# Two reciprocals of a linear-attention layer: one VectorE instruction each in place of two on ScalarE

## The chip, the core and the metric

The kernel runs on one core of a Trainium2 chip. The metric is the device time of one execution in microseconds (us). The engines are named as in the profile: PE is TensorE's matmuls and PEld its weight loads, DVE is VectorE, ACT is ScalarE, POOL is GpSimd, and SP is the engine that issues most of the transfers. Each engine has its own queue and runs it in order; a semaphore holds an instruction back until what it reads is there.

## The reference

Four layers are applied in turn to `x` (2048 rows of 512, bf16), A B A B, each as `x = x + layer(layernorm(x))`. Layer A is a linear attention with 32 heads of 16:

```
pq = einsum("bhsd,hdf->bhsf", q, w_phi);  pk likewise
phi_q = concat[softmax(pq), softmax(-pq)]      # 32 features a head
phi_k = concat[softmax(pk), softmax(-pk)]
kv  = einsum("bhsf,bhsd->bhfd", phi_k, v);  z = einsum("bhsf->bhf", phi_k)
num = einsum("bhqf,bhfd->bhqd", phi_q, kv)
den = einsum("bhqf,bhf->bhq", phi_q, z) + 1e-6
o = num / den;  return o @ wo
```

Layer B is a sliding attention over 8 positions that lie 2 apart (logits, softmax, weighted sum of v, `@ wo`). The change touches layer A alone: the divisor of the query's softmax (the query normaliser) and `den` (the denominator).

## The kernel before

The 2048 rows are four blocks of 512 (`b` = 0 to 3), and layers A and B exist twice (`L` = 0, 1). The class `_Fast` builds every layer from short steps. For layer A these are:

- `s_a1`: keys and values of a block; exponentials `Ek` on ACT (L599), their sums over 16 features on DVE (L626 to L639), the reciprocal `rk` on ACT (L645, L646), the scaling of `Ek` on DVE (L651), and the sum over all rows into `kv` on PE (L668).
- `s_a2`: queries of a block; `mq` (L698) and the exponentials `Eq` of both signs on ACT (L706). `ms` (L714) sums the exponentials of a head into the PSUM tile `S`, 128 partitions by 2 signs times 128 rows, and `rs` (L718 to L722) makes `rS` = 1/S of it, f32.
- `s_akv`: once a layer, when all four blocks have added to `kv`: it is copied (L190 on DVE or L192 on ACT), transposed (L744) and masked into `ZM` and `R` on DVE (L753, L757).
- `s_a3`: `md` (L782) multiplies the exponentials by `ZM` into a PSUM tile; `dr` (L787 to L793) multiplies it by `rS` (L790) and adds the two signs (L793) into `Ds`; `ln` (L795 to L797) makes 1/(Ds + 1e-6); `rho` (L799 to L801) is the product of `rS` and that, which scales the exponentials of the query: for blocks 0 and 1 through PE (`bc`, L808, into PSUM) and DVE (`mulp`, L816), for blocks 2 and 3 through DRAM (`wr`, `rdb`) and DVE (`muld`, L835).
- `s_a4`: `num` on PE (`mo`, L900), its evictions (L190, L192), the product with `wo` (L520), the residual (L533 on DVE, or L523 with L530 on ACT), the squares for the next normalisation (L540), and the normalisation itself (L428 to L444).

Both reciprocals are exp(-ln(x)) on ACT. No step runs in the order in which it is written: a table of 1452 entries, `_ORDER`, says which step is issued next. It fixes the queue of every engine, so the place of a step in the table is its place in the queue of whichever engine it names. The tables `_SLOTS` fix which of 8 PSUM banks and which SBUF buffers each tile takes, so a step also waits until the bank's previous reader is done.

In the table, the four `rs` steps of the first layer A stand behind the scaling of `Ek` of block 2 (block 0), behind `rho` of block 0 (block 1), among the `mulp` of block 1 (block 2) and behind three normalisations L444 of block 0 (block 3). Those of the second layer A stand behind the L651 of block 1 (block 0), behind the sums of block 2 (block 1), between the copy of `kv` and `ZM` (block 2) and among the `mulp` of block 0 (block 3). `ln` stands close behind `dr` each time: directly so for block 0 in both layers, and then `rho` follows at once.

Of the kernel before, what the change touches and what calls it, by code (L numbers as in the profile page):

```python
# [11 lines left out]
ALU = mybir.AluOpType  # L12
ACT = mybir.ActivationFunctionType
# [3 lines left out]
P = 128  # L17
# [8 lines left out]
DEN_EPS = 1e-6  # L26
# [103 lines left out]
class _Fast:  # L130
# [558 lines left out]
    def s_a2(self, L, b):  # L689
        nc, add = self.nc, self.step  # L690
        st = "a2_%d%d" % (L, b)
        T = {}

        def mq(hb):
            xnT = self.xnT["A%d" % L, b]
            T[hb] = pq = self.ps()
            for k in range(NB):
                nc.tensor.matmul(pq[:], lhsT=self.WA[:, k, hb * P:(hb + 1) * P], rhs=xnT[:, :, k, :],  # L698
                                 start=(k == 0), stop=(k == NB - 1))

        def eq(hb, s):
            if (L, b) not in self.Eq:
                self.Eq[L, b] = {}
            if s not in self.Eq[L, b]:
                self.Eq[L, b][s] = self.med([4, NB, P], "Eq")
            nc.scalar.activation(out=self.Eq[L, b][s][:, :, hb, :], in_=T[hb][:].rearrange("p (t i) -> p t i", t=4),  # L706
                                 func=ACT.Exp, scale=1.0 - 2.0 * s)

        def ms():
            T["S"] = S = self.ps()  # L710
            for s in range(2):
                for hb in range(NB):
                    for t in range(4):
                        nc.tensor.matmul(S[32 * t:32 * t + 32, s * P:(s + 1) * P], lhsT=self.indS[:, hb, :],  # L714
                                         rhs=self.Eq[L, b][s][:, t, hb, :], start=(hb == 0 and s == 0),
                                         stop=(hb == NB - 1), tile_position=(0, 32 * t), skip_group_check=True)

        def rs():  # L718
            r = self.sm([2, P], "rS", F32, 4)
            nc.scalar.activation(out=r[:], in_=T["S"][:, 0:2 * P], func=ACT.Ln)  # L720
            nc.scalar.activation(out=r[:], in_=r[:], func=ACT.Exp, scale=-1.0)
            self.rS[L, b] = r  # L722

        for hb in range(NB):
            add(st, "PE", mq, hb)
            add(st, "ACT", eq, hb, 0)
            add(st, "ACT", eq, hb, 1)
        add(st, "PE", ms)
        add(st, "ACT", rs)

    def s_akv(self, L):
# [39 lines left out]
    def s_a3(self, L, b, dma):  # L771
        nc, add = self.nc, self.step
        st = "a3_%d%d" % (L, b)
        zm = self.ZM[L]
        T = {}
# [11 lines left out]
        def dr():  # L787
            r = self.rS[L, b]
            T["DR"] = self.sm([2, P], "s1", F32, 1)
            nc.vector.tensor_tensor(out=T["DR"][:], in0=T["D"][:, 0:2 * P].rearrange("p (s i) -> p s i", s=2),  # L790
                                    in1=r[:], op=ALU.mult)
            T["Ds"] = self.sm([P], "Ds", F32, 1)
            nc.vector.tensor_tensor(out=T["Ds"][:], in0=T["DR"][:, 0, :], in1=T["DR"][:, 1, :], op=ALU.add)  # L793

        def ln():  # L795
            nc.scalar.activation(out=T["Ds"][:], in_=T["Ds"][:], func=ACT.Ln, bias=self.deneps_t[:, 0:1])
            nc.scalar.activation(out=T["Ds"][:], in_=T["Ds"][:], func=ACT.Exp, scale=-1.0)  # L797

        def rho():  # L799
            T["rho"] = self.sm([2, P], "rho", BF16)  # L800
# [35 lines left out]

        add(st, "PE", md)
        add(st, "DVE", dr)
        add(st, "ACT", ln)
        add(st, "DVE", rho)  # L840
        def bev(s, t, direct):
# [397 lines left out]
class _Layout:  # L1239
# [6 lines left out]
    def add(self, name, nelem, nbuf=1):  # L1246
        self.regions[name] = (self.off, nelem, nbuf)
        self.off += nelem * nbuf
        return self
# [568 lines left out]
```

## Time and profile before

| | before |
|---|---|
| device time, median of two runs | 329.95 us (329.52 to 330.39) |
| span of the profiled execution | 327.5 us |
| its own time, taken as the span and the 2.45 us by which the median exceeds it | 329.95 us |
| mean granted TensorE clock | 0.998 |
| busy: PE / DVE / ACT / POOL | 310.3 / 302.2 / 279.3 / 25.3 us |

The span runs from the first to the last instruction of the profiled execution; what starts and ends an execution lies around it. "Busy" is the time in which an engine has an instruction under way. Two layers A take about 0 to 85 us and 170 to 230 us, with parts of layers B beside them; the rest is layer B. A row of the groups gives the source line, engine, operation, output and inputs, their shapes, the count, the busy sum in us and the mean in ns, and behind the last bar the idle time of the engine just before these instructions, with what ended it. A row of the timeline gives the start in us, the length in us and then the same, with the idle time in brackets.

### The profile page before, as it was taken

How to read it: one execution, taken by the hardware profiler on the slowest of the kernel's cores; microseconds unless marked ns; L12 is line 12 of the kernel's file. 1: busy time of each engine (PE TensorE's matmuls, PEld its weight loads, DVE VectorE, ACT ScalarE, POOL GpSimd, SP SyncE). 2: the span in 40 equal slices, each digit the busy share in tenths (PEclk: the TensorE clock that was granted, in tenths of full speed). 3: DMA queues.
4: the chain of work that ended last, by engine and by line, in shares of the span. 5: the costliest groups of instructions: out<-in, count | busy, mean ns of one | idle time of the engine just before them, and what ended most of it. 6: DMA issues, size and time to landing. Idle time of an engine off the chain costs nothing. (4 is left out here: it accounts for less than half of the span.)

```text
span 327.5 us, 8033 instructions
## 1 busy us (share of the span) xinstructions
PE 310.3 (95%) x3176; PEld 149.5 (46%) x3203; DVE 302.2 (92%) x439; ACT 279.3 (85%) x634; POOL 25.3 (8%) x50
## 2 busy tenths in 40 slices
PE   7999999999999999999999999979999999999873
PEld 3655456445444444443444455644544454433221
DVE  7998995998998999899999999699999999999993
ACT  5999988998888999989999999798999996676550
POOL 4000000000021003000000000000000208400000
PEclk9999999999999999999999999999999999999999
DMA  7980000004556899998750300023436977679952
GB/s 197 380 197 3 0 2 4 2 20 120 105 148 135 152 164 133 139 121 154 137 135 1 67 3 2 4 59 90 128 58 125 179 146 134 150 139 158 166 176 92
DMA packets 37388, 35.41 MB, mean 108 GB/s; under 512 B 23008, under 2 KB 32224, under 8 KB 37344
## 3 DMA queue, kind: packets, MB, share of 16 engines
q1 hardware_dynamic: 36816, 34.81, 53.6%
q8 instruction: 27, 0.44, 0.6%
q14 instruction: 17, 0.14, 0.2%
q10 hardware_dynamic: 528, 0.02, 0.1%
HBM read 10.50 MB, written 2.36 MB: 39 GB/s over the span
## 5 line engine op out<-in xcount | busy, mean ns | idle before, releaser
L927 PE MATMUL ps<-xnT,WB 128*128 128x512 bf16 x384 | 87.6, 380 | 0.5 <-DMA xnT<-xn 0.5
L1081 DVE TENSOR_TENSOR pav<-PT,Vg 128x4096 bf16<-128x4096 bf16 (+1 forms) x34 | 72.0, 2162 | 1.5 <-DMA Vg<-V 1.0
L1019 DVE TENSOR_TENSOR prod<-QT,K 128x4096 bf16<-128x4096 bf16 x32 | 72.5, 2291 | 0.3 <-ACT QT L192 0.2
L927 PEld LDWEIGHTS <-WB 128*128 128x128 bf16 x384 | 42.3, 114 | 43.3 <-issue 5.8
L520 PEld LDWEIGHTS <-oT 128*128 128x128 bf16 x256 | 23.8, 97 | 34.5 <-ACT oT L192 5.7
L192 ACT CAST oT<-ps 128x512 bf16<-128x512 f32 (+1 forms) x60 | 32.1, 587 | 8.4 <-PE ps L1090 7.1
L706 ACT ACTIVATE Eq<-ps 128x512 bf16<-128x512 f32 x64 | 34.0, 615 | 0.7 <-PE ps L698 0.6
L520 PE MATMUL ps<-WoB,oT 128*128 128x512 bf16 x122 | 32.1, 380 | 2.4 <-ACT oT L192 2.0
L599 ACT ACTIVATE Ek<-ps 128x512 bf16<-128x512 f32 x64 | 33.6, 622 | 0.4 <-PE ps L593 0.2
L698 PE MATMUL ps<-xnT,WA 128*128 128x512 bf16 x128 | 30.7, 380 | 0.6 <-DVE Eq L816 0.6
L540 ACT ACTIVATE sqd<-x 128x512 bf16<-128x512 bf16 x48 | 30.1, 643 | 1.0 <-DVE x L533 0.8
L605 PE MATMUL ps<-WA,xnT 128*128 128x512 bf16 x120 | 30.0, 380 | 0.5 <-issue 0.2
L593 PE MATMUL ps<-WA,xnT 128*128 128x512 bf16 x124 | 29.7, 380 | 0.6 <-DMA xnT<-xn 0.2
L520 PE MATMUL ps<-WoA,oT 128*128 128x512 bf16 x120 | 29.2, 380 | 0.4
L533 DVE SCALAR_TENSOR_TENSOR x<-ps,x 128x512 bf16<-128x512 f32 x38 | 25.4, 686 | 1.9 <-PE ps L520 1.7
L192 ACT CAST V<-ps 128x512 bf16<-128x512 f32 x31 | 17.5, 595 | 4.4 <-PE ps L927 4.3
L192 ACT CAST K<-ps 128x512 bf16<-128x512 f32 x31 | 17.8, 585 | 3.7 <-PE ps L927 3.3
L530 ACT ACTIVATE x<-ps 128x512 bf16<-128x512 f32 x26 | 15.1, 598 | 6.4 <-PE ps L523 6.3
L192 ACT CAST QT<-ps 128x512 bf16<-128x512 f32 x29 | 17.1, 592 | 2.5 <-PE ps L927 2.5
L651 DVE TENSOR_TENSOR Ek<-Ek,rk 128x4096 bf16<-128x4096 bf16 (+1 forms) x10 | 18.6, 1858 | 0.5 <-ACT rk L646 0.5
L593 PEld LDWEIGHTS <-xnT 128*128 128x128 bf16 x128 | 12.1, 97 | 15.4 <-DMA xnT<-xn 0.7
L446 ACT ACTIVATE xn<-x,nmr,rstd 128x512 bf16<-128x512 bf16 x23 | 18.2, 822 | 1.0 <-DVE nmr L435 0.8
(129 smaller groups left out, 433.3 us busy)
## 6 DMA issues: line engine op xcount, KB each, us to landing
Vg<-V SPq DMA_DIRECT2D x128, 131.5 KB, 4.4
Prho<-rd SPq DMA_DIRECT2D x8, 512.0 KB
x<-in_A_x_dram SPq DMA_DIRECT2D x3, 512.0 KB
WB<-in_B_wqkv_dram SPq DMA_DIRECT2D x3, 512.0 KB, 11.6
wraw<-in_A_wqkv_dram SPq DMA_DIRECT2D x4, 256.0 KB, 4.5
out_dram<-x SPq DMA_DIRECT2D x4, 256.0 KB, 2.2
out_dram<-x SPq DMA_DIRECT2D x8, 128.0 KB, 2.2
x<-in_A_x_dram SPq DMA_DIRECT2D x4, 128.0 KB
```

The lines of the kernel that those rows point to most:

```text
L192: self.nc.scalar.copy(out=out, in_=in_)
L520: nc.tensor.matmul(y[:], lhsT=oT[:, c, t * P:(t + 1) * P], rhs=Wo()[:, c, :], start=(c == 0), stop=(c == NB - 1 and not onpe))
L533: nc.vector.scalar_tensor_tensor(out=xb[:, t, :], in0=T[t][:], scalar=1.0, in1=xb[:, t, :], op0=ALU.mult, op1=ALU.add, **kw)
L540: nc.scalar.activation(out=sqd[:], in_=xb[:, t, :], func=ACT.Square, accum_out=T["ss"][:, t:t + 1])
L593: nc.tensor.matmul(pk[:], lhsT=xnT[:, t, k, :], rhs=self.WA[:, k, D:2 * D], start=(k == 0), stop=(k == NB - 1))
L599: nc.scalar.activation(out=T["E"][:, t, s, :], in_=T["k", t][:], func=ACT.Exp, scale=1.0 - 2.0 * s)
L605: nc.tensor.matmul(pv[:], lhsT=xnT[:, t, k, :], rhs=self.WA[:, k, 2 * D:3 * D], start=(k == 0), stop=(k == NB - 1))
L698: nc.tensor.matmul(pq[:], lhsT=self.WA[:, k, hb * P:(hb + 1) * P], rhs=xnT[:, :, k, :], start=(k == 0), stop=(k == NB - 1))
L706: nc.scalar.activation(out=self.Eq[L, b][s][:, :, hb, :], in_=T[hb][:].rearrange("p (t i) -> p t i", t=4), func=ACT.Exp, scale=1.0 - 2.0 * s)
L927: nc.tensor.matmul(pp[:], lhsT=self.WB[:, k, i * D + c:(i + 1) * D:NB], rhs=xnT[:, :, k, :], start=(k == 0), stop=(k == NB - 1))
L1019: nc.vector.tensor_tensor(out=pr[:], in0=QT[:, c:c + 1, :].to_broadcast([P, NW, TB]), in1=win, op=ALU.mult)
L1081: nc.vector.tensor_tensor(out=pv, in0=PT[:, :, lo:lo + n].unsqueeze(1).to_broadcast([P, NB, 2, n]), in1=vw, op=ALU.mult)
```

## The change

`rs` becomes one DVE reciprocal that reads PSUM, and `ln` one DVE reciprocal in place. The 1e-6, which was the bias of the logarithm, moves into the DVE addition in front of it, which becomes a scalar_tensor_tensor. The order table, the buffers and everything else stay as they are.

```diff
         def rs():
             r = self.sm([2, P], "rS", F32, 4)
-            nc.scalar.activation(out=r[:], in_=T["S"][:, 0:2 * P], func=ACT.Ln)
-            nc.scalar.activation(out=r[:], in_=r[:], func=ACT.Exp, scale=-1.0)
+            nc.vector.reciprocal(r[:].rearrange("p s i -> p (s i)"), T["S"][:, 0:2 * P])
             self.rS[L, b] = r
...
             T["Ds"] = self.sm([P], "Ds", F32, 1)
-            nc.vector.tensor_tensor(out=T["Ds"][:], in0=T["DR"][:, 0, :], in1=T["DR"][:, 1, :], op=ALU.add)
+            nc.vector.scalar_tensor_tensor(out=T["Ds"][:], in0=T["DR"][:, 0, :], scalar=DEN_EPS, in1=T["DR"][:, 1, :],
+                                           op0=ALU.add, op1=ALU.add)
 
         def ln():
-            nc.scalar.activation(out=T["Ds"][:], in_=T["Ds"][:], func=ACT.Ln, bias=self.deneps_t[:, 0:1])
-            nc.scalar.activation(out=T["Ds"][:], in_=T["Ds"][:], func=ACT.Exp, scale=-1.0)
+            nc.vector.reciprocal(T["Ds"][:], T["Ds"][:])
```

## The prediction

> **What bounds the kernel now.** I read the busy shares first, then the stretches of layer A, then the groups of the edited lines, then DVE's timeline around each place where a new instruction will stand. The page's busy line and four of the answer by stretches (columns: stretch in us, its length, busy us and instructions of PE, PEld, DVE, ACT, POOL, clock, DMA share, GB/s):
>
> ```profile
> PE 310.3 (95%) x3176; PEld 149.5 (46%) x3203; DVE 302.2 (92%) x439; ACT 279.3 (85%) x634; POOL 25.3 (8%) x50
> ...
> 40.00:60.00 20.00, 19.45 (x473) 11.26 (x473) 15.68 (x28) 17.33 (x40) 0.38 (x1) 1.00 0.01 2
> 60.00:80.00 20.00, 19.68 (x303) 9.96 (x304) 18.41 (x46) 18.89 (x46) 0.00 (x0) 1.00 0.21 53
> ...
> 180.00:200.00 20.00, 19.79 (x267) 10.60 (x268) 19.40 (x38) 19.74 (x47) 0.38 (x1) 1.00 0.15 29
> 200.00:210.00 10.00, 9.54 (x243) 5.82 (x246) 7.86 (x12) 8.68 (x20) 0.00 (x0) 1.00 0.02 3
> ```
>
> Three engines run nearly full side by side. DVE is idle for 327.5 - 302.2 = 25.3 us in all, of which 3.7 us lie before 40 us (17.58 and 18.69 us busy of 20 each) and 5.6 us behind 300 us (21.93 of 27.5), where this change puts nothing. That leaves 16 us. PE is as full, so a delay of DVE that reaches PE can hardly be made up. ACT is the emptiest of the three, and it is the one relieved.
>
> **What goes.** The edited lines, in the groups by line:
>
> ```profile
> L790 DVE TENSOR_TENSOR s<-ps,rS 128x256 f32<-128x256 f32 x8 | 3.4, 421 | 1.7 <-PE ps L782 1.5 <-ACT oT L192 0.2
> L721 ACT ACTIVATE rS<-rS 128x256 f32<-128x256 f32 x8 | 3.3, 417 | 0.3
> L796 ACT ACTIVATE Ds<-Ds,deneps_t 128x128 f32<-128x128 f32 x8 | 3.3, 409 | 1.7 <-DVE Ds L793 1.7
> L720 ACT ACTIVATE rS<-ps 128x256 f32<-128x256 f32 x8 | 3.1, 386 | 0.0
> L797 ACT ACTIVATE Ds<-Ds 128x128 f32<-128x128 f32 x8 | 2.5, 309 | 0.3
> L793 DVE TENSOR_TENSOR Ds<-s 128x128 f32<-128x128 f32 x8 | 2.3, 292 | 0.3
> ```
>
> ACT loses 3.1 + 3.3 + 3.3 + 2.5 = 12.2 us. I price that at nothing by itself, since more than half of the 48 us that ACT is idle (25 us, in its evictions L192 and L530) waits for PE; it is counted only where DVE waited for ACT, below. L793 becomes a scalar_tensor_tensor: the two operations cost the same where both appear (L550 159 ns, L552 166 ns on 4 elements; L533 686, L816 682 ns on 512), so nothing.
>
> **What comes: sixteen DVE reciprocals, whose price no row shows.** DVE's f32 rows go from 292 ns for 128 elements to 421 ns for 256: 1.0 ns an element and 0.16 us fixed. That is one pass, and the lower end: 0.42 us for 256 elements and 0.29 us for 128, 8 x 0.71 = 5.7 us in all. But a quotient is no product. [...] I take eight as my estimate: 0.16 + 8 x 0.256 = 2.2 us and 0.16 + 8 x 0.128 = 1.2 us. The long DVE rows lie there too, 2.29 us (L1019) and 1.22 us (L835), and are my upper end: 8 x 3.51 = 28.1 us. Taken: 8 x (2.2 + 1.2) = 27.2 us. I choose near the upper row because nothing in DVE's rows makes a division in one pass.
>
> [...]
>
> **Where they land.** The order table stays, so each reciprocal takes ACT's old place in the order, now in DVE's queue, and everything behind it on DVE moves back unless DVE was idle there. DVE's timeline, first layer A:
>
> ```profile
> 47.04 2.28 DVE L651 TENSOR_TENSOR Ek<-Ek,rk 128x4096 bf16<-128x4096 bf16 x1
> 49.87 1.22 DVE L651 TENSOR_TENSOR Ek<-Ek,rk 128x2048 bf16<-128x2048 bf16 x1 [0.54 <-ACT rk L646]
> ...
> 55.53 0.29 DVE L793 TENSOR_TENSOR Ds<-s 128x128 f32<-128x128 f32 x1
> 56.63 0.42 DVE L801 TENSOR_TENSOR rho<-rS,Ds 128x256 bf16<-128x256 f32 x1 [0.81 <-ACT Ds L797]
> 57.51 0.42 DVE L790 TENSOR_TENSOR s<-ps,rS 128x256 f32<-128x256 f32 x1 [0.46 <-PE ps L782]
> 57.97 0.29 DVE L793 TENSOR_TENSOR Ds<-s 128x128 f32<-128x128 f32 x1
> 58.17 1.28 DVE L816 TENSOR_TENSOR Eq<-ps,Eq 128x512 bf16<-128x512 f32 x2
> ```
>
> Block by block, "rs" being 2.2 us and "ln" 1.2 us:
> - rs 0 stands between the two L651. The 0.54 us wait covers a part: +1.7. The last matmuls of `kv`, then L744, `ZM`, L782 and `dr` hang on that second L651, so it is exposed.
> - ln 0 replaces the trip to ACT, 0.81 us of DVE idle: +0.4.
> - rs 1 stands between `rho` and the next L790, less the 0.46 us wait: +1.7. ln 1 stands ahead of L816, with no idle time: +1.2. Behind both wait the `mulp`, which free PSUM banks that PE needs for L698 and L808.
> - rs 2 (about 65.7 us, DVE without a gap): +2.2. ln 2, with 0.11 us of idle in front of `rho` at 68.94 us: +1.1.
> - ACT, rid of its share, finishes the squares sooner, for which DVE waited 0.80 us at 74.29 us: -0.7.
> - rs 3 stands in front of the copy of `xnT` at 77.20 us, for which PE's L927 waits, less 0.28 us: +1.9. ln 3, before `rho` at 80.41 us: +1.2.
>
> Sum of the first layer: 10.7 us. The second, same view:
>
> ```profile
> 206.73 0.69 DVE L190 CAST vaug<-ps 128x512 bf16<-128x512 f32 x1
> 209.28 0.29 DVE L753 TENSOR_TENSOR ZM<-ps,maskH 128x32 bf16<-128x32 bf16 x2 [1.87 <-PE ps L744]
> ```
>
> - rs 0 (about 191.9 us) and rs 1 (about 199.9 us) stand where DVE has no gap: 4.4. The cast that ends at 207.42 us feeds the last of L668, which ends at 208.17 us; some 0.4 us of that is slack: +4.0.
> - rs 2 stands in front of `ZM`, inside the 1.87 us wait; but its input, the last L714, ends at 208.73 us, so of the wait only 0.55 us is of use: +1.65. Behind it are `ZM` and then L782 on PE.
> - ln 0, as before: +0.4. ln 2 +1.2. ln 1 +1.1 (a gap of 0.1 us). rs 3, whose `S` is ready at 217.78 us, hardly before DVE is: +2.2. ln 3 +1.2.
>
> Sum: 11.75 us. Together 22.45 us; of the 27.2 us on DVE, 4.75 us are hidden. Between 100 and 200 us DVE is idle for 2.9 us and PE for 1.3 us, and I let that win back 1.5 us: **+21 us**. The profiled execution's own time is its span and 2.45 us around it, which is the median of the two runs: 327.5 + 2.45 + 21 = **351 us**. No DMA is issued, but `wr` of blocks 2 and 3 waits for `rho` and starts with the delay already counted.
>
> **Rivals.**
> - *One pass* (the other side). If a reciprocal runs at the rate of the other f32 rows, it fits nearly into the waits it meets: 0.42 us into 0.54, 0.46 and 0.55 us, while ln 0 saves 0.5 us each time; what is left is about 0.3 or 0.4 us at each of the other places less 1 us of ACT's relief, together some +1 us: 331 us. For it: every DVE row is one pass or less per element, and ACT is full from 180 to 200 us (19.74 of 20). [...] Each pass costs 8 x 0.384 = 3.1 us of DVE; from about three passes on, the kernel is slower by 2%. Chance 0.14, with 0.03 of it for ACT's relief weighing more, over 2% faster.
> - *DVE's idle time takes it.* All 16 us of idle time between 40 and 300 us are filled: 27.2 - 16 = +11, 341 us. For it: those 16 us exist. Against it: most are waits for PE, which waits for DVE in turn. Chance 0.15.
> - *The order no longer fits.* PE's order was laid out for ACT doing this beside DVE; banks come free in another rhythm, and nothing is hidden, with 3 us lost besides: 28 + 3, 361 us. Against it: in layer A, PE has L698 to fill with. Chance 0.06.
>
> **How the numbers follow.** The forecast has 0.65. Its own ends: nothing hidden and the upper price gives 329.95 + 28.1 = 358 us; four passes (1.18 and 0.67 us, 14.8 in all) less the 6.25 us hidden or won back gives 338.5 us. The range 338 to 358 us takes in the second rival and leaves out the first and third, 0.2. Two per cent, 6.6 us, is about what a measurement of this kernel tells from no change. Slower by more: 0.65 + 0.15 + 0.06 = 0.86; within: 0.11; faster: 0.03.
>
> **What will show it.** A DVE reciprocal row of 128x256 with a mean near 2200 ns, and one of 128x128 near 1200; DVE busy near 329 us and ACT near 267; PE's idle time up from 17 to nearly 40 us, with waits for DVE at L668, L698, L782 and L808; the first layer A some 11 us longer and the second 12, the layers B unchanged. A reciprocal row near 420 ns makes the forecast wrong at its root; a row near 2200 ns with a span under 341 us means the idle time took more than I counted.

## The result, and the profile after

The changed kernel takes 347.6 us (347.41 to 347.79), the kernel before 329.95: slower by 5.3%, ratio 1.0526, 95% interval 1.0477 to 1.0576. The forecast was 351 us in a range of 338 to 358. The profiled execution spans 345.7 us, 18.2 more than the one before. The medians differ by less, 17.65 us, because the profiled execution before was a quick one: an execution takes some 1.7 us beyond its span (347.41 against 345.7 us here) and not the 2.45 us of the forecast, so that one took about 329.2 us. The forecast's sum is not touched by this, since it starts from the median.

The busy line of the page after:

```profile
span 345.7 us, 8020 instructions
...
PE 316.3 (92%) x3176; PEld 151.2 (44%) x3203; DVE 321.6 (93%) x455; ACT 271.1 (78%) x602; POOL 25.3 (7%) x50
```

DVE's busy time rose by 19.4 us and the span by 18.2 us. ACT's fell by 8.2 us and not by the 12.2 us of the removed rows: the lengths of its other rows are unchanged within 0.6 us in all, but neighbouring rows overlap (before, their lengths add up to 338.5 us against 279.3 us busy), and busy time counts an overlap once. PE's busy time rose by 6 us though it executes the same 3176 matmuls, which the forecast had no reason for.

The edited lines of the kernel after, in the groups by line (the change removes one line at 721, so everything behind has a number one smaller):

```profile
L720 DVE RECIPROCAL rS<-ps 128x256 f32<-128x256 f32 x8 | 14.0, 1752 | 1.1 <-PE ps L714 1.1
L796 DVE RECIPROCAL Ds<-Ds 128x128 f32<-128x128 f32 x8 | 7.6, 949 | 0.2
...
L789 DVE TENSOR_TENSOR s<-ps,rS 128x256 f32<-128x256 f32 x8 | 3.4, 421 | 1.8 <-PE ps L781 1.7
L800 DVE TENSOR_TENSOR rho<-rS,Ds 128x256 bf16<-128x256 f32 x8 | 3.3, 417 | 0.1
...
L792 DVE SCALAR_TENSOR_TENSOR Ds<-s 128x128 f32<-128x128 f32 x8 | 2.3, 292 | 0.3
```

A reciprocal of 256 elements takes 1752 ns and one of 128 takes 949 ns, 14.0 + 7.6 = 21.6 us in all. The multiplications next to them take 421 and 417 ns, as before, and L792, now with the added constant, 292 ns, as before. Of the 1.7 us of idle time in front of `rho` (L801 before, 1.6 of them waits for ACT), 0.1 are left.

DVE's timeline after, where the forecast's first steps lie:

```profile
49.27 1.75 DVE L720 RECIPROCAL rS<-ps 128x256 f32<-128x256 f32 x1
50.94 1.16 DVE L651 TENSOR_TENSOR Ek<-Ek,rk 128x2048 bf16<-128x2048 bf16 x1
...
56.53 0.29 DVE L792 SCALAR_TENSOR_TENSOR Ds<-s 128x128 f32<-128x128 f32 x1
56.85 0.95 DVE L796 RECIPROCAL Ds<-Ds 128x128 f32<-128x128 f32 x1
57.84 0.42 DVE L800 TENSOR_TENSOR rho<-rS,Ds 128x256 bf16<-128x256 f32 x1
58.19 1.75 DVE L720 RECIPROCAL rS<-ps 128x256 f32<-128x256 f32 x1
60.04 0.42 DVE L789 TENSOR_TENSOR s<-ps,rS 128x256 f32<-128x256 f32 x1
```

The waits of 0.54, 0.81 and 0.46 us that stood here before are filled, and from 56.07 to 66 us DVE has no gap of over 0.1 us. The second L651 starts 1.07 us later than before (49.87), `rho` 1.21 us later (56.63), the second L789 2.53 us later (57.51). Taking the same difference in front of and behind each new instruction gives the table; "priced again" is the forecast's step with 1.75 and 0.95 us in place of 2.2 and 1.2.

| step | first layer A: forecast | priced again | measured | second: forecast | priced again | measured |
|---|---|---|---|---|---|---|
| rs 0 | 1.7 | 1.2 | 1.1 | 4.0 (with rs 1) | 3.1 | 3.2 |
| ln 0 | 0.4 | 0.15 | 0.2 | 0.4 | 0.15 | 0.2 |
| rs 1 | 1.7 | 1.3 | 1.3 | (above) | | |
| ln 1 | 1.2 | 0.95 | 1.0 | 1.1 | 0.85 | 0.8 |
| rs 2 | 2.2 | 1.75 | 1.7 | 1.65 | 1.2 | 0.9 |
| ln 2 | 1.1 | 0.85 | 0.7 | 1.2 | 0.95 | 0.95 |
| ACT's relief | -0.7 | -0.7 | -0.2 | | | |
| rs 3 | 1.9 | 1.45 | 1.1 | 2.2 | 1.75 | 1.7 |
| ln 3 | 1.2 | 0.95 | 1.0 | 1.2 | 0.95 | 0.9 |
| not in the forecast | | | 1.7 | | | 1.0 |
| all | 10.7 | 7.9 | 9.3 | 11.75 | 8.95 | 9.3 |

Small differences of DVE's overlap, up to 0.1 us each, are in the sums alone. After the first layer 0.7 us of the 9.3 was won back (8.6 us from 109 us on), and the second starts from 8.9: 8.9 + 9.3 = 18.2 us.

The row "not in the forecast" is the growth of DVE's waits for PE in, or just behind, stretches in which TensorE's granted clock is low. The stretches of the kernel after, with the prediction's columns (busy us of PE, PEld, DVE, ACT, POOL, then the clock):

```profile
60.20:63.60 3.40, 1.24 (x18) 0.68 (x18) 3.33 (x7) 1.35 (x3) 0.00 (x0) 0.99 0.02 5
63.60:67.00 3.40, 3.40 (x9) 1.22 (x8) 2.38 (x5) 2.06 (x4) 0.00 (x0) 0.50 0.00 0
...
227.40:230.80 3.40, 1.99 (x39) 0.99 (x42) 3.37 (x8) 1.71 (x4) 0.00 (x0) 1.00 0.10 19
230.80:241.00 10.20, 7.84 (x123) 3.73 (x124) 9.53 (x18) 4.75 (x10) 0.00 (x0) 0.50 0.40 104
```

Before, the granted clock stood at 1.00 through layer A. Here PE is busy for only 1.24 of 3.4 us while DVE works through rs 1 and ln 1, and in the next 3.4 us the clock is 0.50. PE's timeline shows the price: twelve matmuls L698 that took 2.75 us before (first row) take 4.44 us, and DVE, which waited 0.11 us at this place before, waits 1.79 us for the L807 behind them.

```profile
59.51 2.75 PE L698 MATMUL ps<-xnT,WA 128*128 128x512 bf16 x12 [0.22 <-DVE Eq L816]
```

```profile
62.37 0.38 PE L807 MATMUL ps<-rho,indB 32*128 32x128 bf16 x13 [1.63 <-DVE Eq L815]
62.97 4.44 PE L698 MATMUL ps<-xnT,WA 128*128 128x512 bf16 x12 [0.21 <-DVE Eq L815]
```

```profile
67.77 1.89 DVE L815 TENSOR_TENSOR Eq<-ps,Eq 128x512 bf16<-128x512 f32 x3 [1.79 <-PE ps L807]
```

So the working theory has two parts. A: DVE's queue pays for the division where each reciprocal stands. C: PE's pauses, which the longer DVE queue causes, bring its clock to half, and that costs a further 2 to 3 us. The rivals were B, that the place in the queue costs and not the division, and D, that the order of PE and ACT sets the time.

### The profile page after: what moved, and what is told of

It is laid out like the page before. It is cut to its first block, busy times and chain, and to the rows that moved or that the text cites. A ratio compares the mean times of both kernels' runs of the same rounds, so it can differ in the third digit from the quotient of the medians.

```text
span 345.7 us, 8020 instructions
## 1 busy us (share of the span) xinstructions
PE 316.3 (92%) x3176; PEld 151.2 (44%) x3203; DVE 321.6 (93%) x455; ACT 271.1 (78%) x602; POOL 25.3 (7%) x50
## 4 chain that ended last, share of the span: by engine, by line
PE 52%; DVE 27%; DMA 7%; ACT 6%; issue 4%; SPq 2%; DVEq 0%; ACTq 0%
PE ps L926 20%; PE ps L520 9%; DVE Ek L651 4%; PE ps L698 4%; DVE rS L720 4%; PE ps L593 4%; DMA xnT<-xn 3%; PE ps L1025 3%; PE ps L1089 2%; DMA Vg<-V 2%; DVE s L626 2%; DVE Eq L815 2%; DVE prod L1018 2%; DVE x L533 2%; PE ps L605 2%
## 5 line engine op out<-in xcount | busy, mean ns | idle before, releaser
L706 ACT ACTIVATE Eq<-ps 128x512 bf16<-128x512 f32 x64 | 34.4, 616 | 10.9 <-PE ps L698 10.7
L698 PE MATMUL ps<-xnT,WA 128*128 128x512 bf16 x128 | 32.3, 396 | 0.7 <-DVE Eq L815 0.7
L520 PE MATMUL ps<-WoA,oT 128*128 128x512 bf16 x120 | 30.4, 391 | 0.6 <-ACT bs L845 0.2
L533 DVE SCALAR_TENSOR_TENSOR x<-ps,x 128x512 bf16<-128x512 f32 x38 | 25.2, 684 | 1.4 <-PE ps L520 1.3
L530 ACT ACTIVATE x<-ps 128x512 bf16<-128x512 f32 x26 | 15.1, 598 | 8.5 <-PE ps L523 8.5
L1089 PE MATMUL ps<-pav,indAV 128*32 128x512 bf16 (+1 forms) x272 | 17.7, 370 | 1.2 <-DVE pav L1080 1.1
L698 PEld LDWEIGHTS <-WA 128*128 128x128 bf16 x128 | 12.0, 101 | 15.4 <-issue 3.6
```

The lines of the kernel that those rows point to most:

```text
L520: nc.tensor.matmul(y[:], lhsT=oT[:, c, t * P:(t + 1) * P], rhs=Wo()[:, c, :], start=(c == 0), stop=(c == NB - 1 and not onpe))
L533: nc.vector.scalar_tensor_tensor(out=xb[:, t, :], in0=T[t][:], scalar=1.0, in1=xb[:, t, :], op0=ALU.mult, op1=ALU.add, **kw)
```

## The experiments

### Is it the division, or its place?

Both reciprocals become a one-pass instruction of the same shape at the same place. It writes a constant (1/16, 1/256), so the division is left out and nothing else.

```diff
-            nc.vector.reciprocal(r[:].rearrange("p s i -> p (s i)"), T["S"][:, 0:2 * P])
+            nc.vector.tensor_scalar(out=r[:].rearrange("p s i -> p (s i)"), in0=T["S"][:, 0:2 * P], scalar1=0.0,
+                                    scalar2=1.0 / 16, op0=ALU.mult, op1=ALU.add)
...
-            nc.vector.reciprocal(T["Ds"][:], T["Ds"][:])
+            nc.vector.tensor_scalar(out=T["Ds"][:], in0=T["Ds"][:], scalar1=0.0, scalar2=1.0 / 256,
+                                    op0=ALU.mult, op1=ALU.add)
```

> Both reciprocals become a one-pass DVE instruction of the same shape and place (times 0, plus 1/16 or 1/256), so the division itself is left out. Theory A, the time is the price of the division (rows of 1752 and 949 ns): rows near 420 and 290 ns, 5.7 us on DVE instead of 21.6, 329 to 333 us. Rival B, the time is the place, ACT's work put into DVE's queue with DVE's order unchanged: 338 us or more even at this price.

331.39 us against 329.63 on the same chip, ratio 1.0051 (1.0028 to 1.0073). Its rows, by line:

```profile
L720 DVE TENSOR_SCALAR rS<-ps 128x256 f32<-128x256 f32 x8 | 3.3, 418 | 1.1 <-PE ps L714 1.1
...
L797 DVE TENSOR_SCALAR Ds<-Ds 128x128 f32<-128x128 f32 x8 | 1.8, 224 | 0.2
```

B falls: at 3.3 + 1.8 = 5.1 us on DVE, moving the work there costs 1.8 us. The other 15.4 us of the change come with the length of the division, what it does to PE's clock included. Even here the trace has one stretch at half clock:

```profile
222.10:225.50 3.40, 3.18 (x19) 1.26 (x20) 3.37 (x8) 1.57 (x4) 0.00 (x0) 0.50 0.49 125
```

Ahead of it the rows of DVE lag by 1.45 us (`rho` of block 3), 0.50 of which stand already in front of the first edited instruction; behind it they lag by 2.74 us (the first L836), so 1.3 us come in this stretch. The forecast's rival of one pass gave the steps some 1 us, and its 0.95 us ahead of the stretch agree; that its 331 us were also the time is in part luck, since the clock was not in its sum.

### Each part alone

In two kernels, only one of the steps has its reciprocal on DVE, and the other stays as before. (The comments in this diff are not in the kernels.)

```diff
+            nc.vector.reciprocal(r[:].rearrange("p s i -> p (s i)"), T["S"][:, 0:2 * P])     # first kernel: only rs
...
+            nc.vector.reciprocal(T["Ds"][:], T["Ds"][:])                                     # second kernel: only ln
```

> Only the normaliser's reciprocal is on DVE (8 of 1752 ns, 14.0 us), the denominator stays on ACT. Theory A, each is paid where it stands, by the shifts of DVE's rows in the changed kernel: about 11 us, 341 us. Rival C, part of the loss comes from PE standing idle so long that its clock is lowered (1.7 us of waiting in the first layer), which needs both parts: 339 us or less, and no stretch with a lower clock.

> Only the denominator's reciprocal is on DVE (8 of 949 ns, 7.6 us), the normaliser stays on ACT. Theory A: by the shifts about 5 to 6 us, 335 us, of which 0.2 us each at the two places where DVE waited 0.81 us for ACT. The two single parts then add up to the 17.6 us of the whole. Rival C: the two parts together give 2 to 3 us less than the whole, because the lower clock comes only with both.

343.1 us (ratio 1.0392, 1.0343 to 1.0440) and 335.56 us (1.0148, 1.0108 to 1.0188), against 329.63. That is +13.5 and +5.9, together 19.4 and not the 17.2 to 17.7 of the whole. Both forms of the expectation missed in this: the parts do not add up, and it is not the whole that has the extra cost. In the first layer neither part has a stretch at half clock, and there the lags of DVE's rows do add up: 4.9 and 2.6 us, 7.5 together, against the 7.6 us of the whole without its 1.7. In the second layer each part alone already has its own stretch (6.8 us from 229.7 us on, and 10.2 us from 220.4 us on), and the two waits for PE that go with it grow by 1.9 and 1.6 us. So the sum of the parts holds 3.5 us of such waits and the whole 2.7, which is 0.8 us of the excess of about 2; the rest is not assigned. The executions of the denominator alone differ with the clock: they took 336.37 and 336.40 us where the mean clock was 0.982 and 0.983, and 334.76 and 334.06 us where it was 0.995 and 0.996. The same instructions took 2.0 us longer where the clock was low for longer; which of the two came first, these figures alone do not say.

### Twice the price

```diff
+            nc.vector.reciprocal(r[:].rearrange("p s i -> p (s i)"), T["S"][:, 0:2 * P])
             nc.vector.reciprocal(r[:].rearrange("p s i -> p (s i)"), T["S"][:, 0:2 * P])
...
+            nc.vector.reciprocal(T["DR"][:, 0, :], T["Ds"][:])
             nc.vector.reciprocal(T["Ds"][:], T["Ds"][:])
```

> Each reciprocal is issued twice. Theory A, no idle time of DVE is left at these places, so the second set costs its whole 21.6 us: 368 to 370 us. If DVE still waits for others there, less: under 365 us. Rival C, PE's pauses grow and the clock stays low longer: over 371 us, with more of the span at the lower clock than the 0.977 on average of the changed kernel.

372.89 us (ratio 1.1299, 1.1270 to 1.1329): 25.3 us above the changed kernel, for 21.6 us more on DVE (14.0 and 7.6 us in the new rows). In sum no idle time hides any of it, and 3.7 us come on top. The page of this kernel has the clock row

```profile
PEclk9999998689899999999999999988699999999999
```

with a mean of 0.956 against 0.977. That is what C expected, though the run does not separate the 3.7 us from what idle time may still have hidden.

### Does the clock cost time of its own?

Here PE is given matmuls that compute nothing new where it stands idle: a first matmul, which starts its sum afresh, is repeated.

```diff
             T[hb] = pq = self.ps()
+            for _ in range({(0, 3, 0): 10, (1, 3, 2): 5}.get((L, b, hb), 0)):
+                nc.tensor.matmul(pq[:], lhsT=self.WA[:, 0, hb * P:(hb + 1) * P], rhs=xnT[:, :, 0, :],
+                                 start=True, stop=True)
...
+            for _ in range({(0, 0): 6, (1, 0): 6}.get((L, b), 0)):
+                nc.tensor.matmul(T[0][0:32, 0:w], lhsT=self.R[0:32, self.reg(0, 0), :],
+                                 rhs=self.Eq[L, b][0][0:32, 0:4 // m, 0, :],
+                                 start=True, stop=True, tile_position=(0, 0))
```

> The changed kernel with matmuls that compute nothing new, put where PE stands idle in it (a first matmul that starts its sum afresh, repeated 10 times in L698 of block 3 in the first layer A and 5 times in the second, 6 times in L899 of block 0 in both). Rival C as it now stands, PE's pauses lower its clock and the slower matmuls then cost time of their own (1.7 us at 63.6 us, some 1 to 2 us at 231 us): the stretches at half clock go, and the time falls by 2 to 3 us to 344.5 to 346 us, though PE has 5 us more to do. Theory A alone, DVE's queue is all there is: 347 to 349 us, whatever the clock.

> The changed kernel itself, for the comparison with the other runs of this chip: 347.6 us, within 1 us.

344.89 us (ratio 1.0456, 1.0413 to 1.0498) against 347.12 us (1.0534, 1.0495 to 1.0572) for the changed kernel on the same chip. With 27 matmuls more, the kernel is faster by 2.2 us by the medians; the two intervals touch. In the padded kernel PE's timeline at the first place is

```profile
59.27 2.33 PE L698 MATMUL ps<-xnT,WA 128*128 128x512 bf16 x10
...
63.57 2.75 PE L701 MATMUL ps<-xnT,WA 128*128 128x512 bf16 x12 [0.22 <-DVE Eq L818]
```

The ten fillers stand where PE was idle, and the twelve matmuls (now L701) take 2.75 us as in the kernel before, not 4.44. The stretch at half clock in the first layer is gone:

```profile
60.70:64.10 3.40, 2.83 (x28) 1.27 (x26) 3.33 (x7) 1.46 (x3) 0.00 (x0) 1.00 0.02 5
64.10:67.50 3.40, 3.31 (x31) 1.40 (x29) 3.29 (x7) 2.97 (x8) 0.00 (x0) 1.00 0.00 0
```

DVE's rows settle it more sharply than the times. At the product in front of which DVE waited 1.79 us, the lag against the kernel before jumps from 3.46 to 5.14 us in the changed kernel; in the padded one it is 4.06 and 4.07 us, and all the other steps of this layer are there as before. The 4.44 - 2.75 = 1.69 us of the twelve matmuls are the same amount: the 1.7 us are the price of the lower clock. The stretch in the second layer stayed, with 6.8 us (10.2 us in the changed kernel, 6.8 us in its repetition), so only half of the expectation held. There the fillers in front of the stretch were small, 32 by 32 where the others are 128 by 128. The next kernel makes them full and adds four:

```diff
-                nc.tensor.matmul(T[0][0:32, 0:w], lhsT=self.R[0:32, self.reg(0, 0), :],
-                                 rhs=self.Eq[L, b][0][0:32, 0:4 // m, 0, :],
-                                 start=True, stop=True, tile_position=(0, 0))
+                nc.tensor.matmul(T[0][:], lhsT=self.kvT[:, 0:P], rhs=self.kvT[:], start=True, stop=True)
...
+            for _ in range(2 if (L, b) == (1, 3) else 0):
+                nc.tensor.matmul(S[:], lhsT=self.kvT[:, 0:P], rhs=self.kvT[:], start=True, stop=True)
...
+            for _ in range(2 if (L, b, s) == (1, 1, 0) else 0):
+                nc.tensor.matmul(pb[0][:], lhsT=self.kvT[:, 0:P], rhs=self.kvT[:], start=True, stop=True)
```

> As the padded kernel, with padding that fills all 128x128 of PE (the first layer A's in L900 too) and four more such matmuls in the second layer A, in front of L714 of block 3 and L808 of block 1. If the lower clock of the second layer A (6.8 us in the padded kernel) comes from PE doing too little in the window before it, it goes, and the time falls by another 1 to 2 us to 342 to 344 us. If the pauses are not its cause, the stretch stays and the time is 345 us or more.

343.69 us against 329.78 (ratio 1.0416, 1.0388 to 1.0444), which is another 1.2 us by the medians, though the two intervals overlap. The stretch in the second layer shrank to 3.4 us and came later:

```profile
231.30:234.70 3.40, 2.31 (x80) 1.25 (x78) 3.23 (x9) 1.92 (x4) 0.00 (x0) 1.00 0.49 146
234.70:238.10 3.40, 3.18 (x13) 1.19 (x10) 3.40 (x7) 1.41 (x4) 0.00 (x0) 0.50 0.23 86
```

From 347.1 to 343.7 us, 3.4 of the 17.2 us thus belong to the clock, at least, and here the two kernels' intervals lie apart. That is more than the 2.7 us of the table, because the padded kernels also win back more behind the first layer: 1.4 us (from 7.6 to 6.2 us in this one) against 0.4 us. Why that goes with the clock was not tried. The rest, some 14 us, is DVE's queue.

### Can ACT's freed time be used?

The changed kernel has ACT idle for 345.7 - 271.1 = 74.6 us. First all evictions of layer A, the copies of rho's broadcast included, go to ACT (`False` in place of the table's choice):

```diff
-            self.flex(st + "v", ev, t)
+            self.flex(st + "v", lambda t_, d: ev(t_, False), t)
...
-                direct = _CHOICE[self.nflex] == "1"
-                self.flex(st, bev, s, t)
+                direct = False
+                self.flex(st, lambda s_, t_, d: bev(s_, t_, False), s, t)
...
-                self.flex(st, ev, r, k, m)
+                self.flex(st, lambda r_, k_, m_, d: ev(r_, k_, m_, False), r, k, m)
```

> The changed kernel, and ACT takes all evictions of layer A that DVE had (values, L900's outputs, and the PSUM copies of rho's broadcast, after which the product on DVE takes 416 instead of 682 ns). Theory A, DVE's queue sets the time in layer A and ACT's freed 12 us lie idle: DVE loses about 25 x 0.27 + 12 x 0.68 = 15 us, of which what lies on DVE's side of the waits comes back, 337 to 343 us. Rival D, PE and the order set it: no gain, 346 us or more.

357.58 us, ratio 1.0842 (1.0814 to 1.0869): 10 us slower than the changed kernel, though DVE has 12 us less to do (309.5 us busy). A missed here, and the form that D gave, no gain, came. The rows of this kernel by line show where much of it went:

```profile
L845 ACT CAST bs<-ps 128x512 bf16<-128x512 f32 x32 | 17.6, 649 | 2.1 <-PE ps L807 2.0
...
L815 DVE TENSOR_TENSOR Eq<-bs,Eq 128x512 bf16<-128x512 bf16 x32 | 12.2, 415 | 13.2 <-ACT bs L845 12.9
```

Each product on DVE now waits for a copy that ACT makes just in front of it: 12.9 us of waiting against 25 x 0.27 = 6.7 us saved. The clock has a share in the 10 us too, which is not separated: it is at half for 13.7 and 10.2 us in the two layers, against 3.4 and 6.8 us in the repetition of the changed kernel. A milder kernel leaves those copies on DVE and moves the plain evictions alone (the first and third hunk above):

> The changed kernel, and ACT takes only the plain evictions of layer A from DVE (values and L900's outputs), not the copies of rho's broadcast, on which DVE waited for ACT 12.9 us in the run before. If ACT's freed time can be used where nothing waits at once: 341 to 345 us. If every trip to ACT in layer A is on the way of the next step, 348 us or more.

350.48 us, ratio 1.0620 (1.0589 to 1.0650), still 3 us slower than the changed kernel on DVE's 6.8 us less. So in layer A a shorter DVE queue does not help by itself: what is moved to ACT stands in ACT's queue among its other work, in an order that was not made for it. DVE's wait for ACT's squares grows from 0.9 to 4.1 us, its wait for PE in front of L533 from 1.3 to 6.0 us, and PE's wait for ACT's copies of `oT` from 2.0 to 3.1 us. ACT's idle time was not free time at these places. Whether another order could use it was not tried.

### A version without the normaliser's reciprocal

Since (1/S0)/(D0/S0 + D1/S1) = S1/(D0 S1 + D1 S0), one copy with the two signs swapped replaces the reciprocal. The 1e-6 is added to a sum that is not normalised, and so weighs less than in the reference.

```diff
-            nc.scalar.activation(out=r[:], in_=T["S"][:, 0:2 * P], func=ACT.Ln)
-            nc.scalar.activation(out=r[:], in_=r[:], func=ACT.Exp, scale=-1.0)
+            sv = T["S"][:, 0:2 * P].rearrange("p (s i) -> p s i", s=2)
+            nc.scalar.copy(out=r[:], in_=sv[:, ::-1, :])
```

> The kernel before, without the normaliser's reciprocal: since (1/S0)/(D0/S0 + D1/S1) = S1/(D0*S1 + D1*S0), one ACT copy with the signs swapped takes the place of logarithm and exponential (the 1e-6 is added to the unnormalised sum). ACT loses 8 x 0.42 = 3.3 us and DVE nothing. Theory A, only DVE's queue and PE count here: 329 to 330 us, no change that can be told. If ACT's relief is worth something in the full stretch from 180 to 200 us: 328 us or less.

329.49 us, ratio to the kernel before 0.9989 (0.9973 to 1.0005). ACT's busy time falls from 279.3 to 276.2 us and DVE's stays at 302.2: no difference that can be told, as A expected. Within that, some 0.9 us at most, ACT's time at these places had no price in the kernel before either.

### What an element costs

The normaliser's reciprocal of blocks 0 to 3 is cut into 1, 2, 4 and 8 pieces.

```diff
-            nc.vector.reciprocal(r[:].rearrange("p s i -> p (s i)"), T["S"][:, 0:2 * P])
+            n = (1, 2, 4, 8)[b]
+            w = 2 * P // n
+            rf = r[:].rearrange("p s i -> p (s i)")
+            for k in range(n):
+                nc.vector.reciprocal(rf[:, k * w:(k + 1) * w], T["S"][:, k * w:(k + 1) * w])
```

> The changed kernel with the normaliser's reciprocal cut into 1, 2, 4 and 8 pieces for blocks 0 to 3. From 1752 ns for 256 elements and 949 for 128: 6.27 ns an element and 0.15 us fixed, so 0.95, 0.55 and 0.35 us for 128, 64 and 32 elements out of PSUM. If the price is a step (by whole blocks of elements) and not a line, other numbers.

```profile
L724 DVE RECIPROCAL rS<-ps 128x32 f32<-128x32 f32 x16 | 3.7, 299 | 0.0
L724 DVE RECIPROCAL rS<-ps 128x64 f32<-128x64 f32 x8 | 3.6, 507 | 1.1 <-PE ps L714 1.1
L724 DVE RECIPROCAL rS<-ps 128x128 f32<-128x128 f32 x4 | 3.5, 920 | 0.0
L724 DVE RECIPROCAL rS<-ps 128x256 f32<-128x256 f32 x2 | 3.5, 1750 | 0.0
```

It is a line: 208 ns for 32 more elements, 413 for 64, 830 for 128, which is 6.5 ns an element, and about 0.09 us fixed. The expected 6.27 and 0.15 came from comparing a reciprocal out of PSUM with one out of SBUF: for 128 elements these take 920 and 948 ns in this kernel. Against the 1.0 ns an element of DVE's other f32 rows (421 ns for 256 elements, 292 for 128) this is 6.5 passes. (One execution, 348.74 us; of its time nothing is concluded.)

## Why the prediction was right

- **What bounds the kernel.** Right: DVE and PE together. ACT's relief of 12.2 us was worth nothing by itself; where DVE had waited for ACT's squares, it was worth 0.2 us of the 0.7 that were counted. The version with the swap shows the same from the other side.
- **The price of the new instruction.** The term that was mis-sized. The eight passes in the sum no run shows; the runs show 6.5, and 1.75 and 0.95 us where the sum has 2.2 and 1.2. That alone takes 8 x 0.7 = 5.6 us off the sum of 22.45. How the engine divides no run shows; the rows show only the price. The choice near the upper end was right, since the lower end gives 331 us, as the one-pass kernel measured.
- **What hides it, step by step.** Priced again, the steps give 7.9 and 8.95 us; without the row that was not in the forecast, 7.6 and 8.3 us were measured. No step of a reciprocal is off by more than 0.4 us; the largest errors, rs 3 of the first layer (0.35 us too much) and ACT's relief (0.5 us too much), nearly cancel. The three waits that were said to be filled (0.54, 0.81, 0.46 us) are filled.
- **What was left out.** The drop of PE's clock, 1.7 us in the first layer and 1.0 in the second by the shifts, and 3.4 us by the padded kernels. The forecast put it at nothing. The third rival had "3 us lost besides" because banks come free in another rhythm; the loss is there, but its cause is PE's clock, which no view of the kernel before could show, since there the clock never fell in layer A.
- **What layer B wins back.** 1.5 us forecast; 0.7 us was won back after the first layer, and 0.3 us of that lost again before the second. In the padded kernels it was 1.4 us.
- **The sum.** 21 - 5.6 (price) - 1.0 (steps) + 2.7 (clock) + 1.1 (won back less) = 18.2 us, the span's difference. That the forecast came as near as 3.4 us is in part luck: errors of opposite sign cancel. Had the price alone been right, it would have been 329.95 + 15.4 = 345.3 us, 2.3 us low, and still in the range. The second padded kernel, in which only 3.4 us at half clock are left, comes nearest to what the working describes: its rows of DVE lag by 15.1 us at the end, against those 15.4.
- **The second rival**, that DVE's idle time takes the work: of 21.6 us, 5.7 were hidden at the steps (21.6 - 7.6 - 8.3) and 0.4 won back, not 16. Waits for PE moved with DVE: the 0.74, 0.57 and 0.75 us in front of the copy of `kv`, of `ZM` and of the first L789 stand there after as before.
- **The other signs.** DVE's busy time of 321.6 us (329 expected) and ACT's of 271.1 (267) follow from the price and from the overlapping rows. PE's idle time rose from 17 to 29 us and not to nearly 40: the added time is shorter, and at half clock the same matmuls keep PE busy for longer (twelve of them for 4.44 us in place of 2.75).

What stays open: exactly what halves the clock. The stretches of 3.4 us ahead of a fall had PE busy for 1.24, 1.99, 2.24 (one-pass kernel) and 2.31 us (second padded kernel), but one of 1.87 us (70.4 to 73.8 us in the kernel after) was followed by full clock, so the busy time by itself does not decide. Nor was it tried how much remains with no fall at all.

## What to carry to other kernels

Price a division on VectorE by its elements, at several times a multiplication (here 1752 against 421 ns), before moving it off an engine that has room; a logarithm and an exponential on ScalarE can be the cheaper reciprocal (here 386 + 417 ns). Work that is added to a full queue comes out at most of its length (here 15.9 of 21.6 us by the steps), and relief on an engine that mostly waits was worth next to nothing here, whether it was used or left. When a delay leaves TensorE with gaps, look at its granted clock in the stretch behind them: the gaps can cost a second time (here 1.69 us on twelve matmuls).

## What the hardware showed that was not expected

Within the layers, the granted clock fell to 0.50 for 3.4, 6.8, 10.2 or (with all evictions on ACT) 13.7 us. Ahead of the falls shown above PE had gaps and was not idle throughout: it was busy for 1.24 to 2.31 us of the 3.4 us before each. A kernel with 31 matmuls that compute nothing new is faster by 3.4 us than the same kernel without them, and executions of one kernel that differ in the clock they got differ by 2.0 us.
